# Attention weights computed with the keys on the partitions, in a kernel of attention and two token mixers

## The chip, the core and the metric

One NeuronCore of a Trainium2 chip runs the whole program. The metric is the device time of one execution in microseconds.

## What is computed

Normalised attention over 4 batches, 12 heads, 448 tokens and 64 channels per head, then two mixing layers on the 4 x 448 x 768 result. Only the attention is touched by the change:

```python
def rmsnorm(x, g):
    rms = np.sqrt(np.mean(x * x, axis=-1, keepdims=True) + 1e-06)
    return x / rms * g
q_n, k_n = (rmsnorm(q, g_q), rmsnorm(k, g_k))
scale = 1.0 / np.sqrt(q.shape[-1])
scores = scale * np.matmul(q_n, k_n.transpose(0, 1, 3, 2))
scores = scores - np.max(scores, axis=-1, keepdims=True)
attn = np.exp(scores)
attn = attn / (np.sum(attn, axis=-1, keepdims=True) + 1e-09)
return np.matmul(attn, v).astype(np.float32)
```

The result goes through `_moe_ref` (a gated layer that mixes the tokens by w_sp) and `_moe2_ref` (a token layer and a channel layer), all in f32.

## The kernel before

**Stages.** `Attention` (line 621) works on 24 pairs of heads, one pair per `slot` (line 860). Six pairs make a batch, and when a batch is done `moe(mp, b)` (line 1049) computes its first mixer: products named vps, ups, sps and xps. Attention of later pairs and the mixers of earlier batches run side by side. After the attention come the token layer (h1ps, u_ps) and the channel layer (h2ps, o_ps). `prepare_v` and `prepare_uo` turn the weights into split form meanwhile (tiles word, wpart, wv, ws).

**Number format.** Most products are split: a value is a rounded half HI and a remainder LO, and three one-pass products (`PASSES`: HI HI, HI LO, LO HI) replace one f32 product. Tiles of type F32R hold such halves. Products of plain f32 tiles are called unsplit here.

**One pair of heads.** P = 128 partitions, S = 448 tokens, C = 4 blocks of T = 112 tokens, D = 64 channels, R = 64 tokens in the last block when tokens are cut by 128. `norms` (663) and `scale` (686) normalise q and k with the tokens on the partitions (tile raw); `transposed` (696) turns them so that the channels of both heads fill the 128 partitions. `scores` (725) makes, per block c of 112 query tokens and per head r, a [112 queries x 448 keys] product on half of the array's rows (64 channels): unsplit for pairs below WHOLE = 8 (tiles called whole), in three passes after that. DVE takes the maximum of each row (nm), and ACT the exponential with nm as bias and the row sum as a second output (e, sums). The queries stand on the partitions, so `turned` (784) transposes e on PE, seven 128 x 112 pieces per block, 28 a pair, and ACT and DVE copy them from PSUM (et). `values` (803) multiplies by v: the 448 keys are contracted in four pieces, two heads at once on half of the array's columns, unsplit (av). The division by the sums is done on e by POOL (`normalise`, 754) from pair AFTER = 10 on; before that the reciprocals are spread, transposed (wide) and multiplied in at the end (`divisors`, 769; tile over). The result leaves as xp, split again.

**What sets the order.** Nothing runs as it is written. `Plan` (line 154) records every operation; `place` (267) schedules them on the five engines by list scheduling with estimated durations, and `issue` (381) writes out the best of eight rounds. Each engine's queue is then in that fixed order, and the helper at line 422 issues every instruction, so that all rows carry one line and are told apart by tile names. PSUM's eight banks are shared among three kinds of tiles, and `OWN` (133) is the number that each kind keeps: sc for scores, tp for transposes, mm for the other products. `parts` tells apart the three forms of PE work: 0 the whole array, 1 half of its rows, 2 half of its columns. A change of form is charged SWITCH, and work of the same form may be drawn forward by NEAR (line 429).

Of the kernel before, what the change touches and what calls it, by code (L numbers as in the profile page):

```python
# [12 lines left out]
F32 = mybir.dt.float32  # L13
# [115 lines left out]
class Banks:  # L129
# [3 lines left out]
    OWN = {"sc": 4, "tp": 2, "mm": 2}  # L133
# [16 lines left out]
class Plan:  # L150
# [116 lines left out]
    def place(self, before, after, lag, weight, tiles=None):  # L267
# [21 lines left out]
        while placed < len(ops):  # L289
# [180 lines left out]
def attention_moe_mixer(  # L470
# [66 lines left out]
    def convert(pool, tag, bufs, raw, rows, n, dst_hi, dst_lo, dims=None, at=None):  # L537
# [63 lines left out]

    def rsqrt(pool, src, n, w, mul, tag, bufs=2, on=None):
# [7 lines left out]
        nc.scalar.activation(y[:n], y[:n], AF.Exp, scale=-0.5)  # L610
        on.tensor_tensor(z[:n], y[:n], y[:n], op=ALU.mult)
# [9 lines left out]
    class Attention:  # L621
# [3 lines left out]
        def __init__(self, stack):  # L625
            self.p = Pool(opened(stack, "attn", side="right"))
            self.raw, self.v32, self.r = {}, {}, {}
            self.qt, self.kt, self.e, self.et, self.av = {}, {}, {}, {}, {}
            self.sums, self.over = {}, {}

        def load(self, i):
# [4 lines left out]
            for r in range(2):  # L636
# [3 lines left out]
            on.dma_start(out=t[:, 1, :, 0], in_=k[b, 2 * j].rearrange("(c p) d -> p c d", p=T))  # L640

            src = k[b, 2 * j + 1]
            on.dma_start(out=t[:R, 1, 0, 1], in_=src[LAST:])
            on.dma_start(out=t[R:, 1, 0, 1], in_=src[:T - R])
            on.dma_start(
                out=t[:, 1, 1:, 1], in_=src[T - R:LAST].rearrange("(c p) d -> p c d", p=T))
# [16 lines left out]
        def norms(self, i):  # L663
# [6 lines left out]
            for h in (slice(0, n // 2), slice(n // 2, n)):  # L670
                if i == 0 and h.start:
                    sq = p.tile([T, 2, S], F32, tag="e", bufs=EB, name="e").rearrange("p r s -> p (r s)")
                    sq = sq[:, :n // 2 * D].rearrange("p (n d) -> p n d", d=D)
# [12 lines left out]
        def scale(self, i):  # L686
# [3 lines left out]
            for a in range(2):  # L690
                on = nc.gpsimd if i else nc.vector
                raw = self.raw[i][:, a].rearrange("p c r d -> p (c r) d")
                roots = self.r[i][a][:T]
                on.tensor_tensor(raw, raw, roots.unsqueeze(2).to_broadcast([T, 2 * C, D]), op=ALU.mult)

        def transposed(self, i, a):
# [7 lines left out]
            if i < WHOLE:  # L704
                to = self.qt if a == 0 else self.kt
# [780 lines left out]
```

## Time and profile before

| | |
|---|---|
| time, median of 3 runs | 891.25 us (890.48 to 892.96) |
| profiled execution | 892.5 us |
| its span | 890.7 us, PE clock 0.996 |
| PE busy | 867.3 us, 97% |
| DVE / ACT / POOL busy | 684.7 / 538.3 / 416.7 us |

Busy times overlap at the ends of instructions, since one starts before its predecessor's result is out; the distance from one start to the next is what an instruction costs its engine. An unsplit f32 product of 448 columns leaves two records, a one-pass product and a transpose leave one. Pairs are counted from 0.

### The profile page before, as it was taken

The numbers are of one execution on the slowest core, as the hardware profiler recorded it, in microseconds if no ns is written. First come the engines' busy times: TensorE is split into PE (matmuls) and PEld (weight loads), VectorE is DVE, ScalarE is ACT, GpSimd is POOL, SyncE is SP. The second block draws the span as 40 slices with busy tenths as digits, with TensorE's granted clock in tenths as the row PEclk, the third lists the DMA queues.
The fourth block names the chain that finished last, engine by engine and source line by source line (L and its number), as shares of the span: only waits on it lengthen the run. The fifth ranks groups of instructions, "written<-read, shape, count | busy, mean of one in ns | idle before, by whom it ended". The sixth has DMA issues, their size and how long they took to land.

```text
span 890.7 us, 15921 instructions
## 1 busy us (share of the span) xinstructions
PE 867.3 (97%) x5186; PEld 721.6 (81%) x5186; DVE 684.7 (77%) x1333; ACT 538.3 (60%) x1292; POOL 416.7 (47%) x541
## 2 busy tenths in 40 slices
PE   7898999999999999999999999999999999999998
PEld 5444567787777787777789999999988899999998
DVE  4799897877877867976565466889888886998973
ACT  4999988777876777776543446546324554343331
POOL 3555654795676745665233214234323207524550
PEclk8999999999999999999999999999999999999999
DMA  6555645757535565335687559677564745661441
GB/s 152 154 133 156 193 126 162 203 175 229 162 105 159 151 203 160 90 123 166 211 267 250 178 179 319 194 242 231 157 160 133 230 125 155 213 182 54 142 151 63
DMA packets 149106, 152.30 MB, mean 171 GB/s; under 512 B 77856, under 2 KB 130656, under 8 KB 147488
## 3 DMA queue, kind: packets, MB, share of 16 engines
q1 hardware_dynamic: 148064, 151.06, 56.8%
q8 instruction: 41, 0.67, 0.3%
q14 instruction: 41, 0.34, 0.1%
q10 hardware_dynamic: 960, 0.23, 0.1%
HBM read 112.44 MB, written 38.80 MB: 170 GB/s over the span
## 4 chain that ended last, share of the span: by engine, by line
PE 77%; ACT 9%; DVE 8%; DMA 3%; issue 2%; SPq 0%; POOL 0%; ACTq 0%; DVEq 0%
PE o_ps L422 15%; PE h2ps L422 15%; PE tp L422 8%; PE xps L422 6%; PE ups L422 6%; PE av L422 6%; PE vps L422 5%; PE sc L422 5%; PE sps L422 4%; ACT e L422 4%; PE h1ps L422 3%; PE u_ps L422 3%; ACT et L422 2%; DVE op L422 1%; DVE w L422 1%
## 5 line engine op out<-in xcount | busy, mean ns | idle before, releaser
L422 PE MATMUL h2ps<-op,w 128*128 128x448 f32 x756 | 155.8, 367 | 2.4 <-DVE c L422 2.3
L422 PE MATMUL o_ps<-w,op 128*128 128x384 f32 x882 | 153.6, 334 | 1.2 <-DVE u L422 1.2
L422 PEld LDWEIGHTS o_ps<-w,op 128*128 128x128 f32 x882 | 152.8, 188 | 1.8 <-issue 1.8
L422 PEld LDWEIGHTS h2ps<-op,w 128*128 128x128 f32 x756 | 141.1, 188 | 15.7 <-DVE c L422 4.4
L422 ACT ACTIVATE e<-sc,nm 112x448 f32<-112x448 f32 x192 | 122.5, 653 | 25.3 <-DVE nm L422 25.1
L422 DVE TENSOR_REDUCE nm<-sc 112x1 f32<-112x448 f32 x192 | 109.5, 615 | 17.3 <-PE sc L422 17.0
L422 POOL TENSOR_TENSOR src<-src 128x384 f32<-128x384 f32 x48 | 62.7, 1314 | 77.6 <-DMA src<-c_d 40.6
L422 PEld LDWEIGHTS tp<-ident,e 112*128 112x128 f32 x672 | 71.8, 141 | 32.9 <-ACT et L422 9.3
L422 POOL TENSOR_SCALAR e<-e,sums 112x448 f32<-112x448 f32 x112 | 75.3, 690 | 40.9 <-ACT sq L422 9.7
L422 PE MATMUL tp<-ident,e 112*128 112x112 f32 x672 | 88.7, 262 | 4.6 <-ACT et L422 2.4
L422 ACT ACTIVATE op<-c 128x768 fp32r<-128x768 f32 x49 | 41.5, 847 | 84.6 <-PE o_ps L422 81.2
L422 ACT ACTIVATE et<-tp 128x448 f32<-128x448 f32 x144 | 71.3, 530 | 15.3 <-PE tp L422 14.4
L422 DVE SCALAR_TENSOR_TENSOR word<-raw,word 128x256 uint32<-128x256 uint32 (+2 forms) x132 | 72.2, 553 | 1.4
L422 POOL TENSOR_TENSOR u<-u,o 128x384 f32<-128x384 f32 x28 | 40.2, 1453 | 66.5 <-ACT o L422 35.8
L422 DVE TENSOR_SCALAR word<-word 128x256 f32<-128x256 f32 (+5 forms) x132 | 59.6, 458 | 15.0 <-ACT word L422 14.2
L422 PE MATMUL ups<-xp,wu 128*128 128x448 f32 x288 | 69.1, 376 | 0.0
L422 DVE TENSOR_TENSOR op<-c,op 128x768 fp32r<-128x768 f32 x49 | 57.4, 1172 | 10.3 <-ACT op L422 10.3
L422 PE MATMUL xps<-wo,g 128*128 128x256 f32 x432 | 60.5, 289 | 0.0
L422 PE MATMUL vps<-wv,xp 128*128 128x512 f32 x216 | 59.7, 409 | 0.0
L422 PE MATMUL av<-et,v 128*64 128x448 f32 x288 | 59.6, 548 | 0.0
L422 PEld LDWEIGHTS xps<-wo,g 128*128 128x128 f32 x432 | 54.7, 190 | 5.8 <-issue 2.3
L422 DVE TENSOR_TENSOR c<-c,h2ps 128x448 f32<-128x448 f32 x84 | 50.0, 616 | 11.0 <-PE h2ps L422 10.3
(141 smaller groups left out, 1661.9 us busy)
## 6 DMA issues: line engine op xcount, KB each, us to landing
src<-c_d SPq DMA_DIRECT2D x132, 192.0 KB, 3.1
wu<-wu_d SPq DMA_DIRECT2D x16, 768.0 KB, 4.8
wo<-wo_d SPq DMA_DIRECT2D x12, 1024.0 KB, 5.4
raw<-in_moe_w_ch_dram SPq DMA_DIRECT2D x36, 256.0 KB, 3.5
raw<-in_moe_w_ch_dram SPq DMA_DIRECT2D x24, 384.0 KB, 3.7
raw<-in_q_dram SPq DMA_DIRECT2D x48, 112.0 KB, 2.9
u<-u_d SPq DMA_DIRECT2D x28, 192.0 KB, 3.9
out_dram<-u SPq DMA_DIRECT2D x28, 192.0 KB, 2.0
```

Of the source, the lines that this page charges most:

```text
L422: getattr(getattr(self.nc, op.engine), fn)(*args, **kwargs)
```

## The change

The weights are computed with the keys on the partitions, so that they need no transposing.

- `greatest` multiplies the rounded halves of q and k alone (one pass) for each block of queries and head, and DVE takes the row maxima, into one tile nm of [112 x 128] for all blocks. One transpose turns it, and four ACT copies with a mask per partition (rows) spread it to mt: in mt[:, c] only the two partitions of block c (one per head) are not zero.
- `weighted` makes, per block of 128 keys (the last has 64), the transposed scores [keys x 448 queries] in three passes and adds the negative maxima by a product of a tile of ones with mt. ACT takes the exponential straight into the form that `values` needs, with neither bias nor sum.
- The sums over the keys come from products with a tile of -1 (less, lessr): for pairs 0 to 5 over all key blocks, from pair 6 on over an accumulator acc, which POOL (two additions of 128 x 896) and DVE (the remainder) fill. The division is a logarithm and an exponential on ACT, a correction step and a multiplication on DVE.
- All pairs are scored in three passes, so qt and kt are always split. k is scaled by its norms on ACT, eight 64-column copies, instead of POOL (except pair 0).
- k is loaded by two DMAs instead of four, g on ACT's queue instead of SP's. The first weight words wait for kt of pair 0, and norms(1) for those of pair 0. 18 warm-up products instead of 26. OWN keeps three banks for sc instead of four, and PE may stay among half-array forms when it would leave them.

```diff
-    OWN = {"sc": 4, "tp": 2, "mm": 2}
+    OWN = {"sc": 3, "tp": 2, "mm": 2}
...
+                if not near and parts and not ops[i].parts:
+                    near = [x for x in waiting[e] if ops[x[1]].parts and x[0] <= weight[i] + NEAR]
...
+            a.tile.after = list(a.tile.after) + list(wait)
...
+            for r in range(2):
+                on.dma_start(
+                    out=t[:, 1, :, r], in_=k[b, 2 * j + r].rearrange("(c p) d -> p c d", p=T))
...
+                    if i == 1:
...
+                        sq.tile.after = list(sq.tile.after) + powers[:2]
...
                 on = nc.gpsimd if i else nc.vector
                 raw = self.raw[i][:, a].rearrange("p c r d -> p (c r) d")
                 roots = self.r[i][a][:T]
+                if i and a:
+                    for n in range(2 * C):
+                        nc.scalar.activation(raw[:, n], raw[:, n], AF.Copy, scale=roots[:, n:n + 1])
+                    continue
                 on.tensor_tensor(raw, raw, roots.unsqueeze(2).to_broadcast([T, 2 * C, D]), op=ALU.mult)
 
...
-            elif a == 0:
+            if a == 0:
                 qt = self.qt[i] = self.p.tile([P, 2, S], F32R, tag="qt", name="qt")
                 nc.scalar.activation(qt[:, HI], tpf, AF.Copy)
                 nc.vector.tensor_tensor(qt[:, LO], tpf, qt[:, HI].bitcast(F32), op=ALU.subtract)
...
-        def scores(self, i, *cs):
...
+        def greatest(self, i, *cs):
...
+            qt, kt, nm = self.qt[i], self.kt[i], self.nms[i % 2]
             for c in cs:
+                sc = [psum.tile([P, 512], "tp", "s1")[:T, :S] for _ in range(2)]
                 for r in range(2):
+                    me = slice(r * D, (r + 1) * D)
+                    nc.tensor.matmul(
+                        sc[r], qt[me, HI, c * T:(c + 1) * T], kt[me, HI], start=True, stop=True)
                 for r in range(2):
+                    at = r * D + c
+                    nc.vector.reduce_max(nm[:, at:at + 1], sc[r], axis=AX.X, negate=True)
+            if cs[-1] == C - 1:
+                tp = psum.tile([P, 512], "tp", "nmt")[:, :T]
+                nc.tensor.transpose(tp, nm, ident[:T, :T])
+                mt = self.mt[i] = self.p.tile([P, C, T], F32R, tag="mt", bufs=2, name="mt")
+                for c in range(C):
+                    nc.scalar.activation(mt[:, c], tp, AF.Copy, scale=self.rows[:, c:c + 1])
...
+        def weighted(self, i, c):
...
+            p, qt, kt = self.p, self.qt[i], self.kt[i]
+            mt = self.mt[i].rearrange("p c t -> p (c t)")
+            t, m = TOK[c]
+            sc = [psum.tile([P, 512], "sc", "sc")[:m, :S] for _ in range(2)]
+            with nc.joined_up():
+                for n, (x, w) in enumerate(PASSES):
+                    for r in range(2):
+                        me = slice(r * D, (r + 1) * D)
+                        nc.tensor.matmul(sc[r], kt[me, w, t:t + m], qt[me, x], start=n == 0, stop=False)
+                for r in range(2):
+                    me = slice(r * D, (r + 1) * D)
+                    nc.tensor.matmul(sc[r], self.ones[me, :m], mt[me], start=False, stop=True)
+            if m == P:
+                e = p.tile([P, 2, S], F32, tag="et", bufs=EB, name="et")
+                for r in range(2):
+                    nc.scalar.activation(e[:, r], sc[r], AF.Exp)
+            else:
+                e = p.tile([P, S], F32, tag="er", bufs=2, name="er")
+                for r in range(2):
+                    nc.scalar.activation(e[r * R:(r + 1) * R], sc[r], AF.Exp)
+            es = self.et.setdefault(i, [])
+            es.append(e)
+            if c == 0 or i < 6:
...
+            if c == 1:
+                self.acc[i] = p.tile([P, 2, S], F32, tag="acc", bufs=1, name="acc")
+                nc.gpsimd.tensor_tensor(self.acc[i], es[0], es[1], op=ALU.add)
+            elif m == P:
+                nc.gpsimd.tensor_tensor(self.acc[i], self.acc[i], e, op=ALU.add)
+            else:
                 for r in range(2):
+                    a = self.acc[i][r * R:(r + 1) * R, r]
+                    nc.vector.tensor_tensor(a, a, e[r * R:(r + 1) * R], op=ALU.add)
...
-            av = mm_tile("av")
+            av, sm = mm_tile("av"), mm_tile("sm")
             v32, rest = self.v32[i]
+            es, acc = self.et.pop(i), self.acc.pop(i, None)
...
-                        rhs = self.et[i][:, 2 * kc + r if kc < C - 1 else 2 * kc]
+                        rhs = es[kc][:, r] if kc < C - 1 else es[kc]
...
+            parts = [(self.less, acc[:, r]) for r in range(2)] if acc else [
+                (self.less, es[kc][:, r]) for kc in range(C - 1) for r in range(2)] + [
+                (self.lessr[:, r], es[C - 1]) for r in range(2)]
+            for n in range(0, len(parts), 2):
+                with nc.joined_up():
+                    for r in range(2):
+                        nc.tensor.matmul(
+                            sm[r * D:(r + 1) * D, :S], *parts[n + r], start=n == 0, stop=n == len(parts) - 2)
+
+            over = self.p.tile([P, S], F32, tag="over", bufs=1, name="over")
+            step = self.p.tile([P, S], F32, tag="step", bufs=1, name="step")
+            nc.scalar.activation(over, sm[:, :S], AF.Ln, scale=-1.0)
+            nc.scalar.activation(over, over, AF.Exp, scale=-1.0)
+            nc.vector.scalar_tensor_tensor(step, sm[:, :S], 1e-9, over, ALU.subtract, ALU.mult)
+            nc.vector.scalar_tensor_tensor(step, step, 2.0, over, ALU.add, ALU.mult)
+            nc.vector.tensor_tensor(step, av[:, :S], step, op=ALU.mult)
...
+            nc.scalar.activation(x[:, HI], step, AF.Copy)
+            nc.gpsimd.tensor_tensor(x[:, LO], step, x[:, HI].bitcast(F32), op=ALU.subtract)
...
+                nc.scalar.dma_start(out=g[r * D:(r + 1) * D, 0:1], in_=g_q.unsqueeze(1))
+                nc.scalar.dma_start(out=g[r * D:(r + 1) * D, 1:2], in_=g_k.unsqueeze(1))
...
+            self.rows = self.p.tile([P, C], F32, tag="rows", bufs=1, name="rows")
+            nc.vector.tensor_tensor(self.rows, ident[:, :C], ident[:, D:D + C], op=ALU.add)
...
+            self.greatest(0, *range(C))
...
-            self.scores(s, 0)
-            yield
...
+            self.weighted(s, 0)
+            yield
             self.transposed(s + 1, 0)
             yield
-            self.scores(s, 1)
-            self.normalise(s, 0)
             self.transposed(s + 1, 1)
+            yield
+            self.weighted(s, 1)
+            yield
             self.values(s - 1)
             yield
-            self.scores(s, 2)
-            yield
-            self.turned(s, 0)
+            self.greatest(s + 1, 0, 1)
+            self.weighted(s, 2)
+            yield
             self.norms(s + 2)
             yield
-            self.turned(s, 1)
-            yield
-            self.scores(s, 3)
-            self.normalise(s, 2)
+            self.greatest(s + 1, 2, 3)
+            self.weighted(s, 3)
             yield
...
-    WHOLE, AFTER = 8, 10
...
-    WARM = 26
+    WARM = 18
...
+            behind = [] if wait else [op for _, op in at.kt[0].tile.writers]
+            convert(mp, "vr", 2, raw, P, DU, wv[:, HI, j], wv[:, LO, j], wait=behind)
```

**Order on PE in the opening stage, an early pair.** Before: transposes of e stand between score groups (sc) and one unbroken group of value products (av).

```order
L422 MATMUL tp<-ident,e 128x112 x10
L422 MATMUL tp<-ident,raw 128x112 x8
L422 MATMUL av<-et,v_198 64x448 x6
L422 MATMUL av<-et,vrest 64x448 x2
L422 MATMUL tp<-ident,e 128x112 x7
L422 MATMUL sc<-whole 112x448 x4
L422 MATMUL tp<-ident,e 128x112 x7
L422 MATMUL tp<-ident,wide 128x112 x4
L422 MATMUL tp<-ident,e 128x112 x4
```

Now; s_ are the maxima products, sm the sums with less, sc<-mt,ones adds the maxima:

```order
L424 MATMUL sm<-et,less 64x448 x4
L424 MATMUL av<-et,v_207 64x448 x2
L424 MATMUL s_674<-kt,qt 112x448
L424 MATMUL s_678<-kt,qt 112x448
L424 MATMUL s_682<-kt,qt 112x448
L424 MATMUL sc<-qt,kt 128x448 x6
L424 MATMUL sc<-mt,ones 128x448 x2
L424 MATMUL sm<-er,lessr 64x448 x2
L424 MATMUL av<-et,v_207 64x448 x2
L424 MATMUL s_720<-kt,qt 112x448
L424 MATMUL s_724<-kt,qt 112x448
L424 MATMUL s_726<-kt,qt 112x448
```

No transposes of e are left; av and sm are issued in pieces between the products of the next pair.

**Order on PE just behind the first vps products.** Before, e and wide are transposed between mixer products, and two blocks' scores stand together:

```order
L422 MATMUL vps<-wv,xp 128x512 x7
L422 MATMUL tp<-ident,wide 128x112 x4
L422 MATMUL vps<-wv,xp 128x512 x5
L422 MATMUL tp<-ident,e 128x112 x7
L422 MATMUL vps<-wv,xp 128x512 x4
L422 MATMUL tp<-ident,e 128x112 x2
L422 MATMUL vps<-wv,xp 128x512 x2
L422 MATMUL tp<-ident,e 128x112 x5
L422 MATMUL sc<-kt,qt 112x448 x12
```

Now:

```order
L424 MATMUL vps<-wv,xp 128x512 x36
L424 MATMUL sc<-qt,kt 128x448 x6
L424 MATMUL sc<-mt,ones 128x448 x2
L424 MATMUL sc<-qt,kt 128x448 x6
L424 MATMUL sc<-mt,ones 128x448 x2
L424 MATMUL s_1862<-kt,qt 112x448
L424 MATMUL s_1864<-kt,qt 112x448
L424 MATMUL s_1867<-kt,qt 112x448
L424 MATMUL vps<-wv,xr 128x512 x6
L424 MATMUL s_1895<-kt,qt 112x448
L424 MATMUL sc<-qt,kt 128x448 x6
L424 MATMUL sc<-mt,ones 128x448 x2
```

The half-array work comes in more groups, of eight-product blocks and of one or three maxima products.

**Order on DVE at the start.** Before:

```order
L422 TENSOR_REDUCE ss<-sq 112x8
L422 TENSOR_TENSOR raw<-raw,r0y 112x512
L422 TENSOR_TENSOR raw<-raw,r8y 112x512
L422 TENSOR_SCALAR gg<-gg 128x1
L422 COPY whole<-tp 128x448
L422 TENSOR_SCALAR word<-word 128x512 x2
L422 SCALAR_TENSOR_TENSOR word<-raw,word 128x512
L422 TENSOR_REDUCE nm<-sc 112x1 x6
```

Now:

```order
L424 TENSOR_TENSOR raw<-raw,r0y 112x512
L424 TENSOR_TENSOR raw<-raw,r8y 112x512
L424 TENSOR_REDUCE ss<-sq 112x8
L424 TENSOR_TENSOR qt<-tp,qt 128x448
L424 SCALAR_TENSOR_TENSOR kt<-tp,gg,kt 128x448
L424 TENSOR_REDUCE nm<-s_235 112x1
L424 TENSOR_REDUCE nm<-s_238 112x1
```

Six more maxima follow directly. The remainders of qt and kt and all eight maxima of pair 0 now stand ahead of its first exponential, and the weight words behind them.

## Rows read from the trace of the kernel before

**Rows 1.** The page's part 1: busy us (share of the span) xinstructions.
```profile
PE 867.3 (97%) x5186; PEld 721.6 (81%) x5186; DVE 684.7 (77%) x1333; ACT 538.3 (60%) x1292; POOL 416.7 (47%) x541
```

**Rows 2.** Windows: length, busy us (xinstructions) per engine, PE clock, DMA share, GB/s.
```profile
27.00:97.00 70.00, 64.07 (x402) 34.11 (x402) 61.36 (x131) 68.57 (x195) 42.81 (x69) 1.00 0.58 159
100.00:430.00 330.00, 327.34 (x2143) 245.00 (x2142) 258.03 (x615) 247.81 (x679) 206.57 (x320) 1.00 0.54 157
```

**Rows 3.** Timeline of PE: start, duration (us), line, operation, tiles, shapes, count.
```profile
33.62 2.48 PE L422 MATMUL av<-et,v 128*64 128x448 f32 x12
...
97.17 2.48 PE L422 MATMUL av<-et,v 128*64 128x448 f32 x12
...
100.53 0.48 PE L422 MATMUL vps<-wv,xp 128*128 128x512 f32 x1
...
444.20 0.92 PE L422 MATMUL av<-et,vrest 128*64 128x448 f32 x4
```

**Rows 4.** Timeline of PE again, the rows that give prices.
```profile
36.78 0.89 PE L422 MATMUL tp<-ident,e 112*128 112x112 f32 x7
37.60 1.76 PE L422 MATMUL sc<-whole 64*112 64x448 f32 x8
39.29 0.89 PE L422 MATMUL tp<-ident,e 112*128 112x112 f32 x7
...
52.69 1.56 PE L422 MATMUL tp<-ident,e 112*128 112x112 f32 x14
54.18 1.96 PE L422 MATMUL sc<-whole 64*112 64x448 f32 x8
...
129.12 1.47 PE L422 MATMUL sc<-kt,qt 64*112 64x448 f32 x12
130.52 0.79 PE L422 MATMUL tp<-ident,raw 112*128 112x112 f32 x6
...
207.35 0.86 PE L422 MATMUL sc<-kt,qt 64*112 64x448 f32 x6
208.15 0.98 PE L422 MATMUL tp<-ident,e 112*128 112x112 f32 x7
```

**Rows 5.** Timeline of ACT in the opening stage.
```profile
46.06 0.70 ACT L422 ACTIVATE e<-sc,nm 112x448 f32<-112x448 f32 x1
...
46.67 0.61 ACT L422 ACTIVATE whole<-tp 128x448 f32<-128x448 f32 x1
47.10 0.72 ACT L422 ACTIVATE e<-sc,nm 112x448 f32<-112x448 f32 x1
...
47.71 0.72 ACT L422 ACTIVATE whole<-tp,gg 128x448 f32<-128x448 f32 x1
48.23 0.79 ACT L422 ACTIVATE word<-raw 128x512 f32<-128x512 f32 x1
```

**Rows 6.** Groups of ACT by form: xcount | busy us, mean ns | idle.
```profile
L422 ACT ACTIVATE rest<-tg 128x64 fp32r<-128x64 f32 x16 | 4.0, 252 | 0.0
```

**Rows 7.** Groups of DVE by form.
```profile
L422 DVE SCALAR_TENSOR_TENSOR kt<-tp,gg,kt 128x448 fp32r<-128x448 f32 x16 | 10.8, 677 | 3.2 <-ACT kt L422 3.2
L422 DVE TENSOR_TENSOR qt<-tp,qt 128x448 fp32r<-128x448 f32 x16 | 9.9, 619 | 3.2 <-ACT qt L422 3.1
```

**Rows 8.** Timeline of ACT at the start.
```profile
13.89 0.66 ACT L422 ACTIVATE word<-raw 128x512 f32<-128x512 f32 x1 [1.96 <-DMA raw<-in_moe_w_in_dram]
...
17.66 0.64 ACT L422 ACTIVATE e<-sc,nm 112x448 f32<-112x448 f32 x1 [1.71 <-DVE nm L422]
```

**Rows 9.** Timeline of DVE at the start.
```profile
17.00 1.16 DVE L422 TENSOR_REDUCE nm<-sc 112x1 f32<-112x448 f32 x2 [0.80 <-PE sc L422]
```

**Rows 10.** Windows at the start, PEclk behind POOL.
```profile
12.00:14.00 2.00, 0.87 (x7) 0.47 (x5) 0.90 (x3) 0.11 (x1) 0.00 (x0) 0.91 0.91 280
...
18.00:20.00 2.00, 2.00 (x6) 0.45 (x4) 1.31 (x3) 1.85 (x7) 0.99 (x1) 0.50 0.76 236
```

**Rows 11.** Groups of POOL by form.
```profile
L422 POOL TENSOR_TENSOR raw<-raw,ry 112x512 f32<-112x512 f32 x46 | 50.6, 1114 | 1.5
```

More of the change, by code (lines that the diff above doesn't have):

```diff
@@ L535, in wdram, with convert @@
         return w.bitcast(U32)
-    def convert(pool, tag, bufs, raw, rows, n, dst_hi, dst_lo, dims=None, at=None):
+    def convert(pool, tag, bufs, raw, rows, n, dst_hi, dst_lo, dims=None, at=None, wait=()):
         if f64:
@@ L600, in mm_tile @@
         return psum.tile([P, 512], "mm", name)
+    powers = []
     def rsqrt(pool, src, n, w, mul, tag, bufs=2, on=None):
@@ L627, in __init__ @@
             self.raw, self.v32, self.r = {}, {}, {}
-            self.qt, self.kt, self.e, self.et, self.av = {}, {}, {}, {}, {}
-            self.sums, self.over = {}, {}
+            self.qt, self.kt, self.mt, self.et, self.acc = {}, {}, {}, {}, {}
         def load(self, i):
@@ L769, in divisors @@
-        def divisors(self, i):
-            p, sums = self.p, self.sums[i][:T]
-            nc.vector.tensor_scalar(sums, sums, 1e-9, None, ALU.add)
-            nc.vector.reciprocal(sums, sums)
-            wide = p.tile([T, 2 * C, D], F32, tag="wide", bufs=1, name="wide")
-            nc.gpsimd.tensor_copy(wide, sums.unsqueeze(2).to_broadcast([T, 2 * C, D]))
-            tp = psum.tile([P, C, T], "tp", "tp")
-            for c in range(C):
-                nc.tensor.transpose(
-                    tp[:, c, :], wide[:, 2 * c:2 * c + 2].rearrange("p r d -> p (r d)"), ident[:T, :T])
-            over = self.over[i] = p.tile([P, S], F32, tag="over", bufs=1, name="over")
-            nc.scalar.activation(over, tp.rearrange("p c t -> p (c t)"), AF.Copy)
@@ L848, in start @@
                 self.rests.append(t)
+            one = self.p.tile([P, 1], F32, tag="one", bufs=1, name="one")
+            nc.gpsimd.memset(one, 1.0)
+            self.ones = self.p.tile([P, P], F32R, tag="ones", bufs=1, name="ones")
+            nc.vector.tensor_copy(self.ones, one.to_broadcast([P, P]))
+            self.less = self.p.tile([P, D], F32, tag="less", bufs=1, name="less")
+            nc.gpsimd.memset(self.less, -1.0)
+            self.lessr = self.p.tile([P, 2, D], F32, tag="lessr", bufs=1, name="lessr")
+            nc.gpsimd.memset(self.lessr, 0.0)
+            for r in range(2):
+                nc.gpsimd.memset(self.lessr[r * R:(r + 1) * R, r], -1.0)
+            self.rows = self.p.tile([P, C], F32, tag="rows", bufs=1, name="rows")
+            nc.vector.tensor_tensor(self.rows, ident[:, :C], ident[:, D:D + C], op=ALU.add)
+            self.nms = []
+            for n in range(2):
+                t = self.p.tile([T, P], F32, tag=f"nm{n}", bufs=1, name="nm")
+                nc.gpsimd.memset(t, 0.0)
+                self.nms.append(t)
             tp = psum.tile([P, 512], "tp", "warm")
```

85 lines of the change are left out of this document (4 added, 81 removed).

## The prediction

> **What bounds the kernel now.** I read the page first: PE is busy for 97% of the span, DVE for 77%, ACT for 60% [rows 1]. That is a mean over unlike stages, so next come the busy times by stretch [rows 2]. Between 27 and 97 us, where only attention runs, ACT is busy for 68.6 of 70 us and PE for 64.1; between 100 and 430 us, where attention runs beside the first token mixers, PE is busy for 327 of 330 us and ACT for 248. So there are two limits: **ACT in the opening stage, PE in the long one**. The timeline of PE fixes the first stage [rows 3]: the value products of pair 0 start at 33.62, those of pair 5 at 97.17, so a pair takes (97.17 - 33.62) / 5 = 12.7 us; the first vps product, with which the PE-bound stage begins, starts at 100.53. PE cannot be filled any better behind that, so there only its amount of work counts.
>
> **Prices on PE**, all from starts of neighbouring rows [rows 4]. Twelve one-pass score matmuls take 129.12 to 130.52 = 1.40 us, six take 207.35 to 208.15 = 0.80: six more cost 0.60, so 0.10 each (two heads run at once, a pair in 0.20), and 0.20 is left per group for entering and leaving the half-array form: 0.10 per changeover. Value products, in unsplit f32 (each leaves two records), take 33.62 to 36.78 = 3.16 for four couples of heads, less 0.20: 0.74 a couple [rows 3, 4]. The unsplit f32 scores agree: (39.29 - 37.60 - 0.20) / 2 = 0.75. Fourteen transposes of e take 52.69 to 54.18 = 1.49, less one changeover: 1.39 / 14 = 0.10 each.
>
> **The change on PE.** Removed per pair: 28 transposes of e (2.8 us), and 24 one-pass score matmuls (2.4) or, for pairs 0 to 7, eight unsplit ones (four couples of 0.75 = 3.0); up to pair 9 also 4 transposes of "wide" (0.4). Added per pair: 8 products for the maxima, 24 for the scores and 8 with ones, 40 x 0.10 = 4.0; one transpose, 0.1; the sums with "less", 0.75 where the accumulator exists (pair 6 on) and 3.0 before. So pairs 0 to 5 go from 6.2 to 7.1 (+0.9), pairs 6 and 7 from 6.2 to 4.85 (-1.35), 8 and 9 from 5.6 to 4.85 (-0.75), the last fourteen from 5.2 to 4.85 (-0.35): for the eighteen that lie in the PE-bound stage, -2.7 - 1.5 - 4.9 = -9.1. Three things give it back. The instruction order holds 148 changeovers of form from the first vps product to the last value product, 105 before: +43 x 0.10 = +4.3. In 37 half-array groups there an odd number of maxima products leaves one head unpaired, half a step each: +3.7. And when vps starts, seven pairs had their scores done before, now six: pair 6's old scores (3.0) lay ahead of that point and of its new work only the maxima (0.8) do, +2.2. Sum: **+1.1 in the PE-bound stage**. At 0.096 instead of 0.10 for a transpose (the old stage has 500 of e) it is +3.1, with unpaired heads free it is -2.6; I take +2.
>
> **The change in the opening stage.** ACT, per pair. Prices from starts [rows 5]: an exponential with its sum read out 46.06 to 46.67 = 0.61, a copy from PSUM 46.67 to 47.10 = 0.43, one with a scale per partition 47.71 to 48.23 = 0.52, so 0.09 more. Away: 8 x 0.61, four copies of et of 448 columns (0.43) and two of three quarters of that (0.32): 2.4, the divisor copy 0.43: 7.7 us. New: eight plain exponentials (nearest the copy) 3.4; four copies of 112 columns, a quarter of 0.43 plus fixed part and scale, 0.25 each: 1.0; eight 64-column scalings of k: the row of 64 columns lasts 0.25 [rows 6], of which some 0.1 overlaps its successor, plus 0.09 for the scale: 0.25 each, 2.0, with 0.1 and 0.34 as bounds; the logarithm and exponential 0.9. Together 7.3: **-0.4 per pair**.
> DVE, per pair: the two remainders of qt and kt (0.62 and 0.68) [rows 7] are now made for every pair, +1.3; three passes of such size (0.62) for the division replace one, +1.2; two copies of et (three quarters of that each) and the small operations on the sums go, -1.3: **+1.2**. PE: +0.9. The old loads of 70 us become, over 5.5 pairs, ACT 68.6 - 2.2 = 66.4, DVE 61.4 + 6.6 = 68.0, PE 64.1 + 5.0 = 69.1. Where one engine was full, three now are. They wait for each other in a ring (maxima on DVE, transposed on PE, copied on ACT, added on PE, exponentiated on ACT), so I do not expect each to reach the share that ACT alone reached: I take 13.0 us for a pair, **+1.5 in five pairs**, with 12.3 and 13.8 as bounds (-2 and +5.5).
> The start: the first exponential begins at 17.66, behind a kt copy that stood behind a wait for a weight's DMA at 13.89 [rows 8]. That wait goes (the words now come behind kt), about 2 us earlier. But ahead of the first weights now stand eight maxima on DVE, two of which take 1.16 us and so 0.58 each [rows 9], 4.6 us, a transpose and four copies, 1.3; one maximum stood there before. That is some 3 us later, net +1 to +3, part of it filled by ACT work that must be done anyway. PE's granted clock is 0.91 at 12 to 14 us and 0.50 (the 1.2 GHz level) at 18 to 20 [rows 10], after the gaps behind the warm-up and the first transposes; eight fewer warm-up products and eight thin maxima products make this no better. I take **+0.5**, bounds -1 and +4.
>
> **What costs nothing.** POOL is busy for 43 of 70 and 207 of 330 us [rows 2]: the scalings of e go (pair 10 on), one of two scalings of raw goes (1.11), two additions of 128x896 come, by that row's 1.11 for 512 columns about 2 us each [rows 11]; off the path, like the fewer DMAs for k on SP and the sq and weight work. In the long stage ACT and DVE have room (248 and 258 of 330 us). That cover fails only if a chain is late, a rival below.
>
> **Sum.** +2 +1.5 +0.5 = +4. The profiled execution took 892.5 us (span 890.7), the median of the runs shown is 891.25; made against the first, 896.5, and against the median **895 us**.
>
> **A rule that speaks against it.** Of the four weight groups of a pair three have 128 key columns and the last has 64; all work on 64 rows. In the rows every change between half-array and full products costs 0.10 [rows 4]; whether a change from 128 to 64 columns within the half-array form costs the same, no row shows. The Trainium skill, TensorEngine Tiling (Array Packing), Key Properties, says that changing the tiling mode, not just the tile, drains TensorE, and lists 64x128 and 64x64 as different modes. By the row alone that step is free; by the rule it is two changeovers more per pair.
>
> **Rivals.** (a) *The opening stage shrinks with ACT.* Three balanced engines in a planned order do fill: 12.3 a pair (-2), the start hidden (-1), unpaired heads free and the old transposes at 0.10 (-2.6): -5.6, **886**. For it: ACT had no gaps for 70 us, so queues can run full; against it: PE and DVE would need 97%. (b) *Nothing measurable*: the early loss and the smaller PE sum cancel, 0 to +2.7 against the median: **892**. (c) *Tile form changes inside a weight group*: two per pair at 0.10, 18 pairs bound by PE: +3.6 on top, **898.5**. (d) *The long stage waits for the maxima chain or for banks*: one bank pair more per pair is in use for sums, scores may keep three instead of four. Old idle on PE there is under 3 us in 330. From 0.3 us lost per pair it decides, 18 x 0.3 = +5.4 on top: **900**. That the work isn't replaced as described I exclude: the order shows no transposes of e left.
>
> **Chances.** My forecast 0.33, (c) 0.08, (d) 0.11, all slower; (b) 0.23; (a) 0.25. A measurement tells about 0.3% (2.7 us) from no change. So slower 0.52, same 0.23, faster 0.25. The likeliest case alone spans 890 to 900; for 8 in 10 the range must take in most of (a) and (d): 885 to 902.
>
> **What would show it.** Right: value products of pair 5 at 98 to 101 us, ACT's share between 27 and 97 below 97% while PE and DVE rise above 92%; one-pass matmuls still 0.10 each; from first vps to last value product 345 to 350 us, where it is 444.20 - 100.53 = 343.7 now [rows 3]. Rival (a): pair 5 before 95 us. (c): a step of about 0.30 instead of 0.20 between the third and fourth weight group. (d): idle time on PE of over 6 us between 100 and 430 with DVE or ACT as releaser. I am wrong if the first stage falls by more than 4 us, or if half-array products show another price at 128 columns than at 112.

## The result, and the profile after

The changed kernel takes **904.5 us** (median of 4 runs, 904.12 to 905.68), the kernel before 891.26 beside it: ratio 1.0145, 95% interval 1.0127 to 1.0163. It is slower by 13 us; the forecast was 895 with 902 as upper end. The direction was right, the size was not.

The page's part 1 of the changed kernel answers to [rows 1]:

```profile
PE 880.0 (97%) x5098; PEld 710.9 (79%) x5098; DVE 722.4 (80%) x1310; ACT 536.1 (59%) x1275; POOL 419.0 (46%) x453
```

The same windows as in [rows 2], of the changed kernel:

```profile
27.00:97.00 70.00, 69.51 (x435) 33.43 (x433) 63.59 (x133) 65.21 (x179) 39.14 (x55) 1.00 0.58 158
100.00:430.00 330.00, 322.42 (x1948) 226.31 (x1947) 279.82 (x562) 238.97 (x655) 199.55 (x232) 1.00 0.52 148
```

In the opening stage ACT is no longer full (98% before, 93% now) and PE is (99%). In the long stage PE, which sets it, is *less* busy than before (322.4 of 330, 327.3 then): it now stands idle for 7.6 us instead of 2.7. DVE has 22 us more to do (258.0 before).

PE's timeline of the changed kernel fixes the stages, as [rows 3] did:

```profile
98.81 0.92 PE L424 MATMUL av<-er,vrest 128*64 128x448 f32 x4
...
100.04 2.37 PE L424 MATMUL vps<-wv,xp 128*128 128x512 f32 x9
...
457.33 0.92 PE L424 MATMUL av<-er,vrest 128*64 128x448 f32 x4
```

The first vps product starts at 100.04, at 100.53 before: the opening and the start cost nothing together. From there to the last value products it is 457.33 - 100.04 = **357.3 us, 343.7 before: +13.6**. The whole loss lies in the long stage. To the end of the last value products there, PE is busy for 341.6 us before (of 344.6, from 100.53) and 350.1 now (of 358.2, from 100.04), and idle for 3.0 and 8.1. So by the profile 8.5 us of the loss are more work on PE and 5.1 are waits.

**What the removed transposes had really cost.** PE's timeline of the kernel *before*, in the long stage:

```profile
222.01 0.83 PE L422 MATMUL tp<-ident,e 112*128 112x112 f32 x7
222.62 2.79 PE L422 MATMUL vps<-wv,xp 128*128 128x512 f32 x11
225.25 0.84 PE L422 MATMUL tp<-ident,e 112*128 112x112 f32 x7
225.85 0.71 PE L422 MATMUL vps<-wv,xp 128*128 128x512 f32 x2
226.40 0.83 PE L422 MATMUL tp<-ident,e 112*128 112x112 f32 x7
227.16 0.66 PE L422 MATMUL sc<-kt,qt 64*112 64x448 f32 x4
```

Seven transposes between vps products take 222.62 - 222.01 = 0.61 and 225.85 - 225.25 = 0.60 us, not 0.70; ahead of a change of form it is 227.16 - 226.40 = 0.76. Groups of three take 0.22 there, so four more cost 0.38, 0.096 each, and the last of a group, if a full-array product follows, only 0.03. In the opening-stage rows where I had taken the price, no such product follows; in the long stage one does so behind 88 of the 102 groups. Added from each group's start to the next start, less PE's idle time, the stage's 504 transposes of e make 44.7 us, where 0.10 each made 50.4. The change saves **5.7 us less** than I counted.

**What PE waits for.** Around 145 us of the changed kernel, the timelines of POOL, DVE and PE:

```profile
144.59 2.11 POOL L424 TENSOR_TENSOR acc<-et 128x896 f32<-128x896 f32 x1
146.90 2.10 POOL L424 TENSOR_TENSOR acc<-acc,et 128x896 f32<-128x896 f32 x1
```

```profile
144.48 2.38 DVE L424 TENSOR_SCALAR wpart<-wpart 128x256 uint32<-128x256 uint32 x1
146.78 0.61 DVE L424 TENSOR_TENSOR step<-av,step 128x448 f32<-128x448 f32 x1
147.31 0.68 DVE L424 BATCH_NORM_STATS2 bs<-vr 128x6 f32<-128x512 f32 x1
147.91 0.60 DVE L424 TENSOR_REDUCE nm<-s 112x1 f32<-112x448 f32 x1
```

```profile
148.57 0.82 PE L424 MATMUL sc<-qt,kt 64*64 64x448 f32 x6 [0.69 <-DVE nm L424]
```

POOL adds two weight blocks for 2.11 us from 144.59. DVE's weight scaling, which lasts 0.28 elsewhere, is held until that is over (144.48 + 2.38 = 146.86); the division and the normalisation stand behind it, then the maximum, and PE waits 0.69 us for that. In the window 125 to 150 us DVE is busy for 24.33 of 25 us (the third busy time of the row); "80%" on the page hides this:

```profile
125.00:150.00 25.00, 23.50 (x138) 14.27 (x134) 24.33 (x53) 18.53 (x46) 15.46 (x14) 1.00 0.40 111
```

In the list of PE's waits between 100 and 430 us DVE ends 5.4 of the 7.4 us, the maxima 2.9 of them (total, number of waits, longest):

```profile
PE xps L424 <- DVE nm L424: 1.5, 1, 1.5
...
PE nmt L424 <- DVE nm L424: 0.7, 1, 0.7
PE sc L424 <- DVE nm L424: 0.7, 1, 0.7
```

### The profile page after: what moved, and what is told of

It is laid out like the page before. It is cut to its first block, busy times and chain, and to the rows that moved or that the text cites. A ratio compares the mean times of both kernels' runs of the same rounds, so it can differ in the third digit from the quotient of the medians.

```text
span 903.5 us, 15465 instructions
## 1 busy us (share of the span) xinstructions
PE 880.0 (97%) x5098; PEld 710.9 (79%) x5098; DVE 722.4 (80%) x1310; ACT 536.1 (59%) x1275; POOL 419.0 (46%) x453
## 4 chain that ended last, share of the span: by engine, by line
PE 81%; DVE 12%; ACT 3%; DMA 2%; issue 2%; SPq 0%; POOL 0%; DVEq 0%; ACTq 0%; POOLq 0%
PE o_ps L424 15%; PE h2ps L424 15%; PE sc L424 7%; PE av L424 7%; PE vps L424 6%; PE xps L424 5%; PE ups L424 5%; PE sps L424 4%; PE h1ps L424 3%; PE s L424 3%; PE u_ps L424 3%; PE tp L424 3%; PE sm L424 3%; DVE nm L424 2%; DVE wpart L424 2%
## 5 line engine op out<-in xcount | busy, mean ns | idle before, releaser
L424 PE MATMUL h2ps<-op,w 128*128 128x448 f32 x756 | 155.7, 367 | 1.4 <-DVE c L424 1.3
L424 PE MATMUL o_ps<-w,op 128*128 128x384 f32 x882 | 153.8, 334 | 1.7 <-DVE u L424 1.7
L424 PEld LDWEIGHTS o_ps<-w,op 128*128 128x128 f32 x882 | 152.8, 188 | 2.5 <-ACT op L424 1.3
L424 PEld LDWEIGHTS h2ps<-op,w 128*128 128x128 f32 x756 | 141.0, 188 | 14.9 <-DVE c L424 1.6
L424 DVE TENSOR_REDUCE nm<-s 112x1 f32<-112x448 f32 x192 | 111.4, 615 | 18.3 <-PE s L424 17.5
L424 POOL TENSOR_TENSOR src<-src 128x384 f32<-128x384 f32 x48 | 61.9, 1300 | 75.5 <-DMA src<-c_d 57.6
L424 ACT ACTIVATE op<-c 128x768 fp32r<-128x768 f32 x49 | 41.5, 847 | 85.0 <-PE o_ps L424 75.3
L424 PE MATMUL sc<-qt,kt 64*128 64x448 f32 (+1 forms) x576 | 87.4, 380 | 1.5 <-ACT xo L424 0.8
L424 ACT ACTIVATE et<-sc 128x448 f32<-128x448 f32 x144 | 70.5, 543 | 18.2 <-PE sc L424 13.2
L424 DVE SCALAR_TENSOR_TENSOR word<-raw,word 128x256 uint32<-128x256 uint32 (+2 forms) x132 | 75.9, 578 | 2.0
L424 DVE TENSOR_SCALAR word<-word 128x256 uint32<-128x256 uint32 (+5 forms) x132 | 57.1, 437 | 23.8 <-ACT word L424 22.8
L424 POOL TENSOR_TENSOR u<-u,o 128x384 f32<-128x384 f32 x28 | 41.2, 1487 | 70.7 <-ACT o L424 40.1
L424 PEld LDWEIGHTS sc<-qt,kt 64*128 64x128 f32 (+1 forms) x576 | 55.2, 174 | 19.0 <-issue 3.8
L424 DVE TENSOR_TENSOR op<-c,op 128x768 fp32r<-128x768 f32 x49 | 57.3, 1169 | 10.3 <-ACT op L424 10.2
L424 PE MATMUL av<-et,v 128*64 128x448 f32 x288 | 65.1, 552 | 0.0
L424 PE MATMUL ups<-xp,wu 128*128 128x448 f32 x288 | 65.1, 371 | 0.0
L424 PE MATMUL xps<-wo,g 128*128 128x256 f32 x432 | 60.1, 289 | 2.0 <-DVE nm L424 2.0
L424 DVE TENSOR_TENSOR c<-c,h2ps 128x448 f32<-128x448 f32 x84 | 50.0, 615 | 14.0 <-PE h2ps L424 13.5
L424 PEld LDWEIGHTS xps<-wo,g 128*128 128x128 f32 x432 | 54.8, 191 | 7.9 <-DVE nm L424 3.6
L424 PEld LDWEIGHTS ups<-xp,wu 128*128 128x128 f32 x288 | 53.0, 188 | 7.2 <-issue 2.4
L424 POOL TENSOR_TENSOR acc<-et 128x896 f32<-128x896 f32 x18 | 40.2, 2236 | 36.7 <-ACT et L424 20.7
L424 PE MATMUL s<-kt,qt 64*112 64x448 f32 x192 | 51.9, 421 | 4.8 <-ACT xo L424 1.2
```

The lines of the kernel that those rows point to most:

```text
L424: getattr(getattr(self.nc, op.engine), fn)(*args, **kwargs)
```

## The experiments

Theory W: PE waits in the long stage on a locally full DVE. Theory P: the loss is PE's own work. A stage is named by its first vps and its last value products, as above.

**1. Maxima over a quarter of the keys, order of the change kept** (the planner's estimate is held at 448 columns).

```diff
-   nc.vector.reduce_max(nm[:, at:at + 1], sc[r], ...)
+   nc.vector.reduce_max(nm[:, at:at + 1], sc[r][:, :T], ...)
```

> Each maximum is taken over the first 112 keys only (a quarter of the columns), everything else and the order of all instructions stays as in the change; so PE does the same work with the same 147 changeovers of form, and DVE is freed of about 8 x 0.35 = 2.8 us per pair. Theory W (PE waits for maxima on a locally full DVE: about 5 to 7 us of the long stage's 13.6 us loss): first vps product to last value product 357.3 -> 350 to 352 us, PE idle there under 3 us, whole run 897 to 900. Theory P (the loss is PE work: transposes of e that were cheaper among mixer products than priced, more changeovers, unpaired heads; waits would only be replaced by others): stage 355 to 357, run 902 to 905.

Measured: 899.98 us, ratio 1.0103 (1.0087 to 1.0119). PE's timeline:

```profile
99.76 2.37 PE L426 MATMUL vps<-wv,xp 128*128 128x512 f32 x9
...
453.71 0.92 PE L426 MATMUL av<-er,vrest 128*64 128x448 f32 x4
```

The stage is 354.0 instead of 357.3, below P's range and above W's; the run is 4.5 shorter, at the upper end of W's range. So waits hold a part, and not all.

**2. The additions to acc narrowed to an eighth, order kept, alone and with 1.**

```diff
-   nc.gpsimd.tensor_tensor(self.acc[i], es[0], es[1], op=ALU.add)
+   nc.gpsimd.tensor_tensor(self.acc[i][:, :, :56], es[0][:, :, :56], es[1][:, :, :56], op=ALU.add)
...
-   parts = [(self.less, acc[:, r]) for r in range(2)] if acc else [
+   parts = [(self.less, es[0][:, r]) for r in range(2)] if acc else [
```

> At the order of the change, the additions to acc (two on POOL, two on DVE per pair from pair 6) cover an eighth of their columns, and the products with less read the first weight block instead of acc, so PE's work is the same and it no longer waits for acc; seven eighths of the sums are left out. DVE is freed of about 1.2 us per pair directly, and of whatever POOL's 2.2 us additions cost it by slowing it. Theory W (locally full DVE makes PE wait): stage 357.3 -> 354 to 355. A rival within it, S (POOL's long additions slow DVE's SBUF instructions: wpart scalings 625 ns now, 503 before): those fall back to some 500 ns, and stage -4 to -5, 352 to 353. Theory P (PE work alone): -1 or less.

> Narrow maxima (112 of 448 keys) and narrow additions together, still at the order of the change: what is left of the long stage is PE's work in this order with DVE and POOL out of the way. If the excess over the forecast (13.6 against 2) is about half waits, the stage comes to 349 to 352, so +5 to +8 over the 343.7 of before. If nearly all of it was waits: 346 or less. If nearly none: 354 or more (thin maxima alone gave 354).

Measured: 900.46 (1.0089, 1.0065 to 1.0113) alone, 896.27 (1.0052, 1.0028 to 1.0075) together. Of narrow additions alone, PE's timeline, and below it, between 100 and 430 us, the DVE group that POOL holds up, in the changed kernel (L424) and here (L428):

```profile
99.93 2.37 PE L428 MATMUL vps<-wv,xp 128*128 128x512 f32 x9
...
451.63 0.92 PE L428 MATMUL av<-er,vrest 128*64 128x448 f32 x4
```

```profile
L424 DVE TENSOR_SCALAR wpart<-wpart 128x256 f32<-128x256 f32 x20 | 12.3, 625 | 5.0 <-ACT wpart L424 5.0
```

```profile
L428 DVE TENSOR_SCALAR wpart<-wpart 128x256 f32<-128x256 f32 x20 | 8.8, 447 | 6.0 <-ACT wpart L428 6.0
```

The stage falls to 351.7, and the same 20 scalings from 625 to 447 ns: POOL's long additions do slow DVE (S within W). How much of the stage's 5.6 us is S isn't separated, since DVE's own additions to acc were shortened too (667 to 233 ns, 32 and 34 of them). In the list of PE's waits between 100 and 430 us no wait ended by nm is left. By the ratios, maxima and additions together are 1.0145 - 1.0052 = 0.0093, **8 us** with some 2.5 either way; what remains over before, 0.0052, is 4.6 us, most likely PE's work. The profiled execution of the run with both took 900.4, more than the 896.27 of the median, and its stage is 351.7 too, with PE idle for 4.4 us in it instead of 8.1. So the runs give the waits 8 us and the profiles some 4 to 5: how the 13 us divide is known to some 3 us.

**3. As 1, but ordered anew.**

> The same narrow maxima (112 of 448 keys), but the planner knows that they are short and orders anew: 122 changeovers instead of 147, 22 odd half-array groups instead of 36. Theory W: the waits go (-6) and the changeovers and odd groups too (-2.5 -1.4): about 894 to 897. Theory P: only the -3.9 of the new order: 899 to 902.

Measured: 891.34 us, ratio 1.0012 (0.9997 to 1.0027), and 446.04 - 104.56 = 341.5 us for the stage. It is lower than either theory had it: between this kernel and that of 1, which has the same maxima in the old order, lie 8.6 us (25 changeovers and 14 odd groups fewer are 3.9 of them by the prices). The stages compare only roughly: here vps starts 4.8 us later, with one pair's 32 score products more done ahead of it. PE's timeline:

```profile
104.56 1.87 PE L424 MATMUL vps<-wv,xp 128*128 128x512 f32 x7
...
446.04 0.92 PE L424 MATMUL av<-er,vrest 128*64 128x448 f32 x4
```

So DVE's load seems to cost twice, as waits and as a worse order. The second isn't shown: it is one order against another, and two kernels below that change the planner alone come to 904.8 and 909.7.

**4. Other ways to relieve DVE, or to save PE's odd groups.** Four kernels, each with one of these edits: heads joined, remainder on POOL, no correction, reciprocal.

```diff
+                with nc.joined_up():
                     for r in range(2):
                         me = slice(r * D, (r + 1) * D)
                         nc.tensor.matmul(sc[r], qt[me, HI, ...], kt[me, HI], start=True, stop=True)
```

```diff
-                    nc.vector.tensor_tensor(a, a, e[r * R:(r + 1) * R], op=ALU.add)
+                    nc.gpsimd.tensor_tensor(a, a, e[r * R:(r + 1) * R], op=ALU.add)
```

```diff
-            nc.vector.scalar_tensor_tensor(step, sm[:, :S], 1e-9, over, ALU.subtract, ALU.mult)
-            nc.vector.scalar_tensor_tensor(step, step, 2.0, over, ALU.add, ALU.mult)
-            nc.vector.tensor_tensor(step, av[:, :S], step, op=ALU.mult)
+            nc.vector.tensor_tensor(step, av[:, :S], over, op=ALU.mult)
```

```diff
-            nc.scalar.activation(over, sm[:, :S], AF.Ln, scale=-1.0)
-            nc.scalar.activation(over, over, AF.Exp, scale=-1.0)
+            nc.vector.reciprocal(over, sm[:, :S])
```

> The two heads' maxima products are issued as one, so no half-array group is odd (36 -> 0, at 0.10 each -3.6 us); the order has 170 changeovers instead of 147 (+2.1 at 0.09). If the unpaired heads cost what was priced: -1.5, 902 to 904; if a lone head costs much more than 0.10: below 900; if DVE's maxima are what counts (theory W), joining changes nothing there or makes both banks wait for the later one: 904 to 908.

> The two 64-row additions of the remainder to acc move from DVE to POOL: DVE is freed of 1.37 us per pair, 25 us in the long stage, POOL gets some 45 us more; 146 changeovers, 32 odd groups. Theory W: DVE's fullest stretches ease, stage -2 to -4, run 900 to 902. Theory P: 903 to 905. If the chain acc -> sums -> value is what PE waits for, the slower additions on POOL cost: 905 to 909.

> The division takes exp(-ln(sum)) as it is, without the two DVE passes that correct it (the reference's quantities, one refinement step left out). DVE is freed of 1.2 us per pair, the order has 140 changeovers instead of 147 and 20 odd half-array groups instead of 36. Theory W+O (DVE's load makes PE wait, and makes the planner's order worse): between the change and the kernel with narrow maxima ordered anew, 896 to 900. Theory P: only the changeovers and odd groups, 902 to 903.

> The division by one reciprocal on DVE from PSUM (products with +1 instead of -1) and one multiplication, instead of logarithm and exponential on ACT and three passes on DVE: DVE one pass less per pair if a reciprocal of 448 columns lasts about as long as the other passes (0.6 us), ACT two less; 150 changeovers, 30 odd groups. Theory W+O: 900 to 903. If the reciprocal lasts several times a pass: DVE gets fuller, 910 or more.

Measured: joined 910.33 (1.0227), remainder on POOL 913.09 (1.0256), no correction 900.86 (1.0102), reciprocal 962.51 (1.0786). Joining shortened nothing, and the run lies above all three expectations: the first vps product comes at 106.74, so the opening stage got longer (the chain from maxima to weights, probably), and the long stage became 465.86 - 106.74 = 359.1. A relief of DVE that loads POOL is none: the stage is 466.25 - 100.53 = 365.7, 8 us more, and the run is worse than any expectation; that fits S, though this run doesn't separate the additions' own duration from it. Leaving out two DVE passes gave 3.6 us, just above W+O's range and below P's. The reciprocal failed on its price; the DVE group:

```profile
L424 DVE RECIPROCAL over<-sm 128x448 f32<-128x448 f32 x24 | 70.8, 2951 | 5.5 <-PE sm L424 5.3
```

**5. Undoing parts of the change**, one in each kernel (the fifth is the kernel before with the form rule, 18 warm-up products and the weight words behind kt, as in the change's diff):

```diff
-    OWN = {"sc": 3, "tp": 2, "mm": 2}
+    OWN = {"sc": 4, "tp": 2, "mm": 2}
```

```diff
-SWITCH, NEAR = 200, 2500
+SWITCH, NEAR = 90, 2500
```

```diff
-                if not near and parts and not ops[i].parts:
-                    near = [x for x in waiting[e] if ops[x[1]].parts and x[0] <= weight[i] + NEAR]
```

```diff
-                if i and a:
-                    for n in range(2 * C):
-                        nc.scalar.activation(raw[:, n], raw[:, n], AF.Copy, scale=roots[:, n:n + 1])
-                    continue
```

> OWN keeps four banks for sc again: 153 changeovers, 20 odd groups. If three banks for sc are what PE waits for (rival d, banks): faster than the change, 895 to 900. If the maxima (tp) and the sums (mm) need the shared bank more: slower, 910 to 920.

> The planner counts 90 ns per changeover of form instead of 200, which is what the starts of rows show; 171 changeovers in its order instead of 147, 30 odd groups. If the order suffered from the wrong price: -3 to -6, 898 to 901. If fewer changeovers are better whatever the planner thinks of them: +2 (24 x 0.09) to +5, 906 to 910.

> The change without the rule that lets PE stay among the half-array forms: 148 changeovers (147 with it), 28 odd groups instead of 36 (-0.8). If the rule carries no part of the loss: 902 to 908, within what ordering anew scatters; if it does: 898 or less.

> k is scaled by POOL again in one instruction per pair instead of eight on ACT: ACT freed of 2 us per pair, POOL 1.1 us more, beside which DVE's SBUF instructions run slower; 147 changeovers, 26 odd groups. If ACT still sets the opening stage: its end comes 5 to 10 us earlier, 895 to 900. If DVE and PE hold it there: no gain, 903 to 910.

> The kernel before with three side edits of the change alone: the rule that lets PE stay among half-array forms, weight words behind kt of pair 0, 18 warm-up products instead of 26. 102 changeovers in the long stage instead of 104. If they are neutral, as both theories say: 890 to 893. If the first weight words behind kt help the start by the 2 us that stood there: 888 to 890; if fewer warm-up products leave the clock low for longer: 893 to 896.

Measured: four banks 918.41 (1.0295), changeovers at 90 ns 909.71 (1.0198), no rule 904.80 (1.0153), k on POOL 919.28 (1.0315), side edits in the kernel before 894.69 (1.0027, 1.0005 to 1.0049). No part of the change that is undone here carries the loss by itself. The side edits aren't quite neutral: in the kernel before they cost 2.4 us (0.4 to 4.4), as fewer warm-up products were to do if they left the clock low. But the first vps product starts 3.6 us earlier there, at 96.89, and the long stage is 445.73 - 96.89 = 348.8, 5.1 longer, so it isn't the start that costs. They may hold part of the long stage's loss; the rule alone doesn't, since the change without it gains nothing. Three banks for sc and the scaling on ACT look like gains within the change, of 14 and 15 us, two runs each and each in an order of its own. With k on POOL the run is above either expectation. Its opening window and first vps product read:

```profile
27.00:97.00 70.00, 66.30 (x418) 33.01 (x416) 61.74 (x121) 53.85 (x133) 41.81 (x56) 0.99 0.52 143
```

```profile
106.59 0.97 PE L424 MATMUL vps<-wv,xp 128*128 128x512 f32 x3
```

ACT has 11 us less to do (53.9 against 65.2) and the opening stage ends 6.5 us *later*, with no engine full (PE, the fullest, 66.3 of 70): not the sum of ACT's work sets it. Latency round the ring of engines is the likely reason; no run shows it by itself. The other 8.4 us are in the long stage (472.26 - 106.59 = 365.7), where POOL scales k as well.

**6. Without the maxima, in both layouts.** The edit in the change is below (cut). In the kernel before, the reductions and the bias of the exponential are left out; the third kernel leaves the correction of 4 out as well.

```diff
 def greatest(self, i, *cs):
     if not 0 <= i < NP:
         return
+    return
...
-    nc.tensor.matmul(sc[r], self.ones[me, :m], mt[me], start=False, stop=True)
```

> The maxima are left out wholly: no products s, no reductions, no transposed nm, no copies mt, no products with ones; the weights are exp of the plain scores. 112 changeovers. PE is freed of 18 x (0.8 + 0.8 + 0.1) = 31 us in the long stage, of 35 x 0.09 = 3 for changeovers and 36 x 0.1 = 4 for odd groups; DVE of 18 x 4.5 = 80. Theory P: stage 357.3 - 38 = 319. Theory W: 6 to 8 less, 311 to 313. It tells what the maxima cost in this layout, not a way to compute the reference in general.

> The kernel before without its maxima (no reductions on DVE, exp without bias): DVE is freed of 4.9 us per pair, PE does the same products and transposes, 98 changeovers in the long stage instead of 104. If the maxima cost little where the queries are on partitions, because PE sets the long stage: 885 to 891. Then the new layout without maxima (860.7) is 25 to 30 us better than the old one without, and the change loses by what the maxima need in it. If the old layout gains 25 or more as well (865 or less), the layout itself is worth nothing and the remaining loss is its own.

> The change without maxima and without the two correcting passes of the division: DVE 80 + 22 us lighter in the long stage, 118 changeovers. If DVE still makes PE wait without the maxima: 855 to 858. If PE's work alone is left: 859 to 862.

Measured: the change without maxima 860.65 (0.965, 0.962 to 0.969), the kernel before without maxima 886.05 (0.9941, 0.9926 to 0.9956), the change without maxima and correction 853.99 (0.9584, 0.9564 to 0.9605). PE's timelines, first the change without maxima, then the kernel before without:

```profile
89.28 1.66 PE L424 MATMUL vps<-wv,xp 128*128 128x512 f32 x6 [1.59 <-DVE step L424]
...
410.22 0.92 PE L424 MATMUL av<-er,vrest 128*64 128x448 f32 x4
```

```profile
93.94 0.94 PE L422 MATMUL vps<-wv,xp 128*128 128x512 f32 x3
...
438.13 0.92 PE L422 MATMUL av<-et,vrest 128*64 128x448 f32 x4
```

The long stage is 320.9 and 344.2 us. In the old layout the maxima cost 4.8 us, since DVE had room beside a PE that was full, and that stage doesn't move (343.7 with them). In the new one they cost 904.5 - 860.65 = **44 us**, of which 24 x 1.7 = 41 is PE's work by the prices. The long stage without them comes near P's 319 and not near W's 311 to 313, for PE still waits there: it is idle for 12.3 us, in a new order. Without the correction as well the run is below both expectations, with PE idle for 6.3 us; that fits waits on DVE which were left even without maxima, though the order is new again. Without them the new layout is 0.965 / 0.9941, 2.9% or 25 us better than the old. So the layout by itself is worth 25 us; the maxima, which in it need products of their own and come back through a transpose, four copies and products with ones, eat more than all of it. Both versions without maxima beat both kernels; they rest on q and k being normed, which keeps the scores small, and are no general replacement.

## Why the prediction was right or wrong

- **"28 transposes of e (2.8 us)" per pair, at 0.10**: mis-sized. The price came from the opening stage; among mixer products seven take 0.60 to 0.61. 5.7 us less is saved. Corrected, the bound-stage sum of +1.1 becomes +6.8, where the forecast took +2; the run with maxima and additions short leaves 4.6 (2.5 to 6.7), and the profile shows 8.5 us more of busy PE.
- **"In the long stage ACT and DVE have room (248 and 258 of 330 us)"**: this step failed. The mean hid stretches where DVE is full, and the reductions in it are what the next weights wait for. Costed at nothing, it was 8 us at the same order by the runs with short maxima and additions (5.1 us more idle time on PE by the profile). That is rival (d), held at 0.11 with 900 us; its sign, PE idle for over 6 us with DVE as releaser, is there (7.6 us in 100 to 430, DVE the releaser of 5.4). The maxima, and what stands ahead of them on DVE, are the cause (short maxima alone gave 4.5 us, short additions alone 4.0). Banks in the way I named them (three for sc) are not: four were worse.
- **"two additions of 128x896 ... off the path"** on POOL: wrong in what they do to DVE. At about 2 us each they were priced well (2.24 and 2.17 on the mean), their hold on some of DVE's SBUF instructions was not priced at all.
- **Opening +1.5, start +0.5**: -0.5 together, near the forecast by luck. ACT's timelines of the changed kernel and, below, of the one before:

```profile
21.61 0.98 ACT L424 ACTIVATE et<-sc 128x448 f32<-128x448 f32 x2 [0.64 <-PE sc L424]
...
86.25 1.40 ACT L424 ACTIVATE et<-sc 128x448 f32<-128x448 f32 x3
```

```profile
77.18 0.63 ACT L422 ACTIVATE e<-sc,nm 112x448 f32<-112x448 f32 x1 [0.19 <-DVE nm L422]
```

  From pair 0's first exponential to pair 5's it is 64.6 us, 12.9 a pair (13.0 forecast), and 59.5 before (from 17.66, [rows 8]); the first one comes 3.95 us later, the upper bound I gave. So five pairs cost 5.1 us and not 1.5 (I had the new rate right and took the old one, 12.7, from the value products), the start 3.95 and not 0.5: together 9.1 at pair 5's first exponential. But from there to the start of its last value products it takes 98.81 - 86.25 = 12.6 us, where before even the first of them stood 97.17 - 77.18 = 20.0 behind [rows 3]; to the first vps product it is 13.8 instead of 23.4. That gives 9.6 us back. I had not counted it; that no transposes and copies of e stand between is the likely reason. Two errors of some nine us cancelled.
- **One-pass products at 0.10, changeovers at 0.10**: held. Rival (c) fell; PE's timeline of the changed kernel around a third and fourth weight group (sc<-mt,ones ends the third; the products s run beside both on the other half of the rows):

```profile
227.61 0.36 PE L424 MATMUL s<-kt,qt 64*112 64x448 f32 x1
227.61 0.36 PE L424 MATMUL sc<-mt,ones 64*128 64x448 f32 x1
227.81 0.36 PE L424 MATMUL s<-kt,qt 64*112 64x448 f32 x1
227.81 0.77 PE L424 MATMUL sc<-qt,kt 64*64 64x448 f32 x5
```

  From 128 columns to 64 the step is 0.20, as within a group. The rule of the Trainium skill, TensorEngine Tiling (Array Packing), Key Properties, that a change of mode drains TensorE, agrees with the 0.10 between full and half-array form here. Between these two widths no such price shows; whether TensorE changes its mode there, no run shows.
- **"odd ... unpaired, +3.7"**: not settled. Joining the heads removed all odd groups but changed the order and the chain, and cost more.

Put into the forecast: 895 + 4.8 (the bound stage's +6.8 instead of +2) + 8 (waits) - 2.5 (opening and start, +2 forecast, -0.5 measured) = 905.3, against 904.5 measured. The agreement is closer than the terms are known.

## What to carry to other kernels

Take the price of work that you remove from the place where it stands: what an instruction costs depends on what follows it. Do not cost work at nothing because its engine has room on the mean; look at the fullest window, and at whether what is queued there releases the engine that sets the time. When a layout moves a reduction onto an axis of its own, price the reduction's whole way back (products, transpose, copies, sums) before the saving: here it was 44 us for the maxima against the 25 that the layout is worth without them.

## What the hardware showed that I had not expected

- While POOL adds two SBUF tiles, some of DVE's instructions that read SBUF are held until POOL's is over, but not all. The scaling from SBUF to SBUF is (0.28 became 2.38 us), and on the mean the step of the correction whose two inputs both lie in SBUF. Maxima from PSUM keep their 615 ns, and a multiplication with one input in PSUM and the statistics bs of one SBUF tile keep theirs, though both ran beside POOL's second addition at 147 us. Of the changed kernel and of the one with narrow additions:

```profile
L424 DVE SCALAR_TENSOR_TENSOR step<-step,over 128x448 f32<-128x448 f32 x17 | 12.7, 749 | 0.1
L428 DVE SCALAR_TENSOR_TENSOR step<-step,over 128x448 f32<-128x448 f32 x17 | 11.4, 673 | 0.1
L424 DVE TENSOR_TENSOR step<-av,step 128x448 f32<-128x448 f32 x17 | 10.4, 614 | 1.0 <-PE av L424 0.9
L428 DVE TENSOR_TENSOR step<-av,step 128x448 f32<-128x448 f32 x17 | 10.4, 615 | 1.0 <-PE av L428 0.9
L424 DVE BATCH_NORM_STATS2 bs<-vr 128x6 f32<-128x512 f32 x12 | 8.2, 684 | 4.2 <-ACT vr L424 4.2
L428 DVE BATCH_NORM_STATS2 bs<-vr 128x6 f32<-128x512 f32 x12 | 8.2, 684 | 8.5 <-ACT vr L428 8.5
```

  The Trainium skill, SBUF — State Buffer, Terms, says that DVE and GpSimd take a shared port pair exclusively and the loser blocks wholly. For the instructions that were held, the rows at 144 us agree.
- A reciprocal on DVE takes 2.95 us for 448 columns, some five times another pass (0.61). The Trainium skill, VectorE: DVE Perf Modes, First, the fixed hardware budget, says that reciprocal runs as an iterated divide with a repeat count of 8, and gives no time; a pass that is several times longer agrees with it in direction.
- Seven transposes ahead of a full-array product take 0.60 us; ahead of a change of form 0.76, of which 0.10 is the change. So the same seven are 0.06 cheaper where a full-array product follows, and short groups gain the most per transpose: three take 0.22, four 0.32 (180.49 to 180.81 us of the kernel before).
